# Two token groups take turns with each half of the dense weights, and the third chunk's decays are transferred, in an mLSTM + dense + MoE kernel

## The chip, the cores and the metric

The kernel runs on one core of a Trainium2 chip. The metric is device time in microseconds (us), the median of 3 runs: 747.91 us before the change (747.22 to 748.08). Engines: TensorE (PE) multiplies matrices, VectorE (DVE) and ScalarE (ACT) work elementwise and read PSUM, GpSimd (POOL) works elementwise on SBUF, SyncE (SP) issues most transfers. Each engine runs its own list of instructions in order, and a program of semaphores makes it wait for the others.

## The reference

Three stages follow one another; the output of each is the input of the next.

```python
for t in range(S):                      # 4 batches, 8 heads, 768 steps, head_dim 40
    m_new = max(f[t] + m, i[t]); f_stab = exp(f[t] + m - m_new); i_stab = exp(i[t] - m_new); m = m_new
    C = f_stab * C + i_stab * outer(v[t], k[t])
    n = f_stab * n + i_stab * k[t]
    y[t] = sigmoid(o[t]) * (C @ q[t]) / max(|n . q[t]|, 1)
x = y as 3072 tokens x 320
x = relu(x @ w_in) ** 2 @ w_out         # 320 x 2048, 2048 x 320
e = argmax(x @ w_gate); p = softmax(x @ w_gate)[e]        # 8 experts
out = p * (relu(x @ w1[e]) @ w2[e])     # 320 x 1024, 1024 x 320
```

All data are float32. The dense weights are stored by the host as packed 64-bit words.

## The kernel before

**Attention.** The 3072 tokens are 24 chunks of 128 (4 batches of 6). `order` puts the first chunks of batches 0, 1 and 2 at the head (AT_ONCE = 3), then the rest batch by batch. Within a chunk the recurrence is written as products: scores of keys with queries (`scores`, line 774, into sp), times the decays Ab (`weigh`, 779), times values (`values`, 787, into pv); for chunks with a predecessor also a product of the queries with the carried state C (`inter`, by `triples`, 713). C is renewed by `update` (713), `update_masked` (813) and `carried` (line 820 on), which takes its factor from decT. `divided`, `gated`, `turned` and `out` finish the chunk; the last two transpose it and split it into high and low columns xh and xl (733, 734).

**Decays.** Ab needs the running sum A of the log gates. `gate_stage` computes it in two parts, the first chunk of each batch (early) and the rest (late), from two loads of the gates (463, 483), and writes it to DRAM (A_d, 508). From the third place on the decays come back by a transfer that spreads one row over 128 partitions (`decays`, 648), and `causal` subtracts and masks them on POOL (669, 670); `decay` takes the exponential on ACT. For the first AT_ONCE chunks `decays_early` builds the same in PSUM with PE instead (656, 660, 662). The carried factors decT go through DRAM as well: eAL, L_d (521 to 523), and three transfers on SP in `carry` (529), the word dt.

**Dense layer.** Eight token groups g of three chunks meet 16 weight slices f; a pair (g, f) is a unit. Its first layer is 8 matmuls 128x384 (line 859, into hp), then ACT squares (867, 868) and DVE forms the low part (876, 879); its second layer is 9 matmuls 128x320 (892 to 894) into three accumulators in PSUM. Group 0 goes through all f, then group 1, and so on (`its`). At the last f of a group `fin` copies the accumulators out on ACT (974) and does the routing.

**Weights.** For each f, `decode` has a load (A, line 546), a rescaling (R, ACT), a type conversion (T, 562 on POOL, 564 on ACT), the sign (S, 574), the words (W, 578), the high part (H, 582) and the low part (L, 585, on POOL or DVE).

**Order.** PLAN is a list of words written by hand: g a piece of the gate stage, A R T S W H L a decoding turn, kv qk de ca cb ea eb vw the preparation of a chunk, sc wa wb va vb and so on the steps of `Main`, l and m the first and second layer of a unit, sa, sb and sbP its late steps (P on POOL), f a number of filler matmuls (1403). Each word issues its instructions at once, so the list sets the order on all engines. It covers 18 first layers and 16 second layers. After it a loop goes on by a pace: `attend`, called twice in each unit, adds STEP = 9/16 half steps of attention, and a chunk has PERIOD = 6 half steps. The five PSUM buffers of `psa` are shared by hp, sp, pv, Ap and the transposes; the keys and queries st, and kvo, have two buffers each, Ab four.

**Experts.** From 520 us on the routed experts run (lines 96 to 374), which the change does not touch.

Of the kernel before, what the change touches and what calls it, by code (L numbers as in the profile page):

```python
# [25 lines left out]
L = 128  # L26
# [28 lines left out]
FETCH = 2  # L55
# [322 lines left out]
def kernel(ctx, tc, qk, q3, kvo, gates, w_io, wg, w12, cst, out, dbg=None):  # L378
# [41 lines left out]
    L_d = dram.tile([HR, NCH], F32, name="L_d")  # L420
# [3 lines left out]
    decT = const.tile([120, 12, NCH], F32, name="decT")  # L424
# [6 lines left out]
    xrl = const.tile([128, 3, XR], F32, name="xrl")  # L431

# [25 lines left out]
    def gate_stage():  # L458
# [25 lines left out]
        yield  # L484

        def columns(src, dst, c0, c1):
            pt = psa.tile([128, 512], F32, tag="a", name="pt")
            for ch in range(c0, c1):
                nc.tensor.transpose(out=pt[:, HR * ch:HR * ch + HR], in_=src[:, L * ch:L * ch + L], identity=ident[0:HR, 0:HR])
            nc.scalar.activation(out=dst[:, c0:c1], in_=pt[:, HR * c0:HR * c1].rearrange("p (c h) -> p c h", h=HR), func=ACTF.Copy)  # L490

        for k, (part, c0, c1) in enumerate(((early, 0, 1), (late, 1, NCH))):
# [18 lines left out]
            if k:  # L511
                columns(c, cT, 0, NCH)
# [94 lines left out]
    class Chunk:  # L607
# [958 lines left out]
```

## Time and profile before

| | |
|---|---|
| median of 3 runs | 747.91 us |
| the profiled execution, its time | 745.5 us |
| its span | 743.7 us |
| PE busy | 731.1 us (98%) |
| weight loads of PE busy | 718.0 us (97%) |
| DVE busy | 500.8 us (67%) |
| ACT busy | 418.1 us (56%) |
| POOL busy | 358.2 us (48%) |
| transfers | 108.99 MB, mean 147 GB/s |

The span goes from the first to the last instruction that the hardware profiler records; the time has what lies around it as well. Busy time is the time in which an engine executes, without register, branch, semaphore and transfer-issuing instructions. Matmuls overlap, so that the durations of single records may add up to more than the time they take together; a row of the chain of waits gives the time that a piece of work holds on the path that ended last. An idle time is put down to what ended it. PE's granted clock is given as a share of its full speed.

### The profile page before, as it was taken

Reading aid. Unit: us, or ns where it says so; the run is one execution under the profiler, and the core shown is the slowest. Engines: PE = TensorE matmul, PEld = TensorE weight load, DVE = VectorE, ACT = ScalarE, POOL = GpSimd, SP = SyncE. Lnnn points to the kernel's source line nnn. Section 1 sums busy time; section 2 is a strip of 40 time slices with the busy share of each in tenths; the row PEclk is TensorE's granted clock in tenths of the full one; section 3 lists DMA queues with packets and bytes.
Section 4 is the critical chain, followed back from the end, with each engine's and each line's share of the span. In section 5 each row is a group of like instructions: output and inputs, shape, how many; then the busy total and the mean of one; then the engine's idle time right before and its main releaser. Section 6 shows DMA issues by size and latency. Waiting matters only on the chain.

```text
span 743.7 us, 14447 instructions
## 1 busy us (share of the span) xinstructions
PE 731.1 (98%) x5198; PEld 718.0 (97%) x5198; DVE 500.8 (67%) x1140; ACT 418.1 (56%) x807; POOL 358.2 (48%) x411
## 2 busy tenths in 40 slices
PE   9999999999999999999999999999999999999996
PEld 6899999999999999999999999999899999999996
DVE  9899874875866776575685664455475767877563
ACT  5687865555455456455455434663374566776553
POOL 8568755555455355265355401531346325666431
PEclk9999999999999999999999999999999999999999
DMA  8788864567354364264364000100297556777610
GB/s 253 230 241 270 244 160 106 144 169 239 102 148 119 87 163 121 56 190 115 92 181 100 25 34 1 34 34 34 82 353 234 145 185 201 254 226 243 183 43 24
DMA packets 55043, 108.99 MB, mean 147 GB/s; under 512 B 6896, under 2 KB 34681, under 8 KB 54834
## 3 DMA queue, kind: packets, MB, share of 16 engines
q1 hardware_dynamic: 50370, 95.88, 44.5%
q0 software_dynamic: 4160, 11.77, 5.0%
q8 instruction: 47, 0.77, 0.4%
q10 hardware_dynamic: 432, 0.29, 0.1%
q14 instruction: 34, 0.28, 0.1%
HBM read 98.69 MB, written 10.86 MB: 147 GB/s over the span
## 4 chain that ended last, share of the span: by engine, by line
PE 95%; DVE 3%; issue 1%; ACT 0%; POOL 0%; POOLq 0%; DVEq 0%; SPq 0%
PE hp L859 25%; PE hp L292 13%; PE acc L892 8%; PE acc L894 8%; PE acc L893 8%; PE pv L787 5%; PE op L311 4%; PE op L313 4%; PE op L312 4%; PE sp L774 4%; PE tp L713 3%; PE lp L957 2%; PE xp L278 1%; PE lpt L948 1%; PE xpt L723 1%; PE apart L1403 1%
## 5 line engine op out<-in xcount | busy, mean ns | idle before, releaser
L641 POOL TENSOR_TENSOR kq<-st,kq 120x256 fp32r<-120x256 f32 x136 | 96.6, 742 | 140.6 <-ACT kq L638 140.6
L892 PE MATMUL acc<-w_h,gh 128*128 128x320 f32 x384 | 125.0, 326 | 0.0
L867 ACT ACTIVATE g<-hp 128x384 f32<-128x384 f32 x128 | 62.3, 487 | 102.9 <-PE hp L859 102.3
L894 PE MATMUL acc<-w_h,gl 128*128 128x320 f32 x384 | 118.6, 309 | 0.0
L893 PE MATMUL acc<-w_l,gh 128*128 128x320 f32 x384 | 118.2, 308 | 0.0
L876 DVE SCALAR_TENSOR_TENSOR hp<-hp,g 128x384 f32<-128x384 f32 x126 | 70.6, 560 | 67.3 <-ACT g L867 67.0
L859 PE MATMUL hp<-xh,w_h 128*128 128x384 f32 x384 | 111.9, 345 | 1.6 <-DVE xh L734 1.6
L261 DVE SCALAR_TENSOR_TENSOR gl<-hp,gh 128x384 fp32r<-128x384 f32 x88 | 48.0, 556 | 59.2 <-ACT gh L231 58.6
L859 PE MATMUL hp<-xh,w_l 128*128 128x384 f32 x384 | 87.4, 335 | 0.0
L859 PE MATMUL hp<-xl,w_h 128*128 128x384 f32 x256 | 86.5, 338 | 0.0
L879 DVE TENSOR_TENSOR gl<-hp,gh 128x384 fp32r<-128x384 f32 x126 | 70.3, 558 | 14.3
L893 PEld LDWEIGHTS acc<-w_l,gh 128*128 128x128 f32 x384 | 72.4, 189 | 0.0
L892 PEld LDWEIGHTS acc<-w_h,gh 128*128 128x128 f32 x384 | 72.4, 188 | 0.0
L894 PEld LDWEIGHTS acc<-w_h,gl 128*128 128x128 f32 x384 | 72.0, 188 | 0.0
L868 ACT ACTIVATE gh<-g 128x384 fp32r<-128x384 f32 x128 | 67.3, 525 | 4.4 <-PE acc L893 0.4
L859 PEld LDWEIGHTS hp<-xh,w_l 128*128 128x128 f32 x384 | 68.9, 188 | 0.0
L859 PEld LDWEIGHTS hp<-xh,w_h 128*128 128x128 f32 x384 | 65.5, 189 | 1.8 <-ACT signs L564 1.8
L231 ACT ACTIVATE gh<-hp 128x384 fp32r<-128x384 f32 x88 | 43.2, 491 | 39.7 <-PE hp L292 38.8
L638 ACT ACTIVATE kq<-st,cs 120x1024 fp32r<-120x1024 f32 x34 | 39.0, 1148 | 33.7 <-PE sp L774 33.7
L174 POOL DMA_INDIRECT out_dram<-ot,idx x34 | 41.8, 1231 | 25.7 <-ACT ot L210 18.5
L676 ACT ACTIVATE Ab<-Ab 128x512 f32<-128x512 f32 x42 | 26.2, 628 | 44.4 <-POOL Ab L670 44.4
L787 PEld LDWEIGHTS pv<-kvo,Ab 128*128 128x128 f32 x384 | 48.4, 191 | 0.5
(291 smaller groups left out, 1837.0 us busy)
## 6 DMA issues: line engine op xcount, KB each, us to landing
st<-in_qk_dram SPq DMA_DIRECT2D x34, 480.0 KB
raw<-in_w_dram SPq DMA_DIRECT2D x30, 512.0 KB, 4.6
kvo<-in_kvo_dram SPq DMA_DIRECT2D x24, 529.0 KB
raw<-in_w_io_dram SPq DMA_DIRECT2D x16, 704.0 KB
Ab<-A_d SPq DMA_DIRECT2D x42, 256.0 KB
raw<-in_w_dram SPq DMA_DIRECT2D x20, 427.0 KB, 3.4
raw<-in_w_dram SPq DMA_DIRECT2D x10, 426.0 KB, 4.7
q<-in_q_dram SPq DMA_DIRECT2D x20, 180.0 KB
```

The source lines that it names most:

```text
L261: e.scalar_tensor_tensor(out=gl[:, j], in0=hp[j % 4], scalar=0.0, in1=gh[:, j].bitcast(F32), op0=ALU.max, op1=ALU.subtract).then_inc(sGL, 1)
L292: m = e.matmul(hp[f % 4][:, 0:w], a, c, start=(n == 0), stop=(n == 7))
L641: nc.gpsimd.tensor_tensor(out=o[:, c], in0=self.st[j][:, c], in1=o[:, c].bitcast(F32), op=ALU.subtract)
L787: nc.tensor.matmul(self.pv[:, hd], d.Ab[r][:, i], d.v[:, hd], start=True, stop=True)
L859: nc.tensor.matmul(hp, a, x, start=(n == 0), stop=(n == 7))
L867: nc.scalar.activation(out=r, in_=hp, func=ACTF.Relu)
L868: nc.scalar.activation(out=gh, in_=r, func=ACTF.Square)
L876: e.scalar_tensor_tensor(out=sq, in0=hp, scalar=0.0, in1=r, op0=ALU.max, op1=ALU.mult)
L879: e.tensor_tensor(out=gl, in0=sq, in1=gh.bitcast(F32), op=ALU.subtract)
L892: nc.tensor.matmul(acc[t][:, 0:DM], gh[:, sl], wh, start=(f == 0), stop=False)
L893: nc.tensor.matmul(acc[t][:, 0:DM], gh[:, sl], wl, start=False, stop=False)
L894: nc.tensor.matmul(acc[t][:, 0:DM], gl[:, sl], wh, start=False, stop=end)
```

## The change

1. The units of groups 0 and 1 (SHARED = 2) come in four blocks of PART = 8: (0, f 0 to 7), (1, f 0 to 7), (0, f 8 to 15), (1, f 8 to 15). At f = 7 of both, ACT copies the accumulators to rows of xr2 or xrl, and at f = 15 DVE adds to these rows what the accumulators then hold.
2. `decays_early` is used for ON_PE = 2 chunks where it was for three; the third chunk's decays come through `decays` and `causal`. For that, the first column block of cT is transposed in the early part of the gate stage.
3. decT is made by a product on DVE (own), one matmul on PE and a copy on ACT, from constants that one more small load brings; L_d and `carry` go.
4. PLAN is written anew and covers 26 first layers and 24 second layers; it has 22 filler matmuls where 21 stood. Up to unit 32 the pace is QUICK = 5/4 a call of `attend`.
5. FETCH, the group at whose first unit the first expert's weights are loaded, is 3 where it was 2.

```diff
-FETCH = 2
+FETCH = 3
+ON_PE = 2
+SHARED, PART, QUICK = 2, 8, 5 / 4
 PLAN = """
-    g0 g1 A0 R0 qk0 g2 g3 A1 kv0 TP0 g4 g5 g6 f7 de0 ea0 g7 eb0 g8 R1 g9 TP1 A2 S0 sc0 de1 th0 g10 W0 vw0 qk1 H0 SA1 ea1 R2 up0 A3 eb1 TP2 g11 wb0 wa0 g12
+    g0 A0 g1 g2 R0 kv0 g3 qk0 g4 TQ0 g5 A1 f7 g6 de0 ea0 f3 g7 g8 g9 qk1 S0 W0 sc0 vw0 eb0 g10 A2 H0 g11 R1 wa0 kv1 wb0 de1 T1 S1 th0 ea1 va0 vb0 eb1 R2
...
-    L_d = dram.tile([HR, NCH], F32, name="L_d")
-    decT = const.tile([120, 12, NCH], F32, name="decT")
+    decT = const.tile([120, 3 * B, NCH - 1], F32, name="decT")
+    rows3, rows12 = xrl[0:HR, 1, 0:120], xrl[0:HR, 1, 120:120 + 3 * B]
+    own = xrl[0:HR, 1, 132:132 + 3 * B * (NCH - 1)].rearrange("p (g c) -> p g c", c=NCH - 1)
...
+        nc.scalar.dma_start(out=xrl[0:HR, 1, 0:120 + 3 * B], in_=cst[0:HR, 521 + TT:])
-        def columns(src, dst, c0, c1):
+        def columns(src, dst, c0, c1, more=None):
...
+            if more:
+                more(pt)
...
             if k:
-                columns(c, cT, 0, NCH)
+                columns(c, cT, 1, NCH)
+            else:
+                columns(c, cT, 0, 1)
...
-        columns(eA, eAT, 1, NCH)
-        eAL = const.tile([HR, NCH], F32, name="eAL")
-        nc.vector.memset(eAL[:, 0:1], 0.0)
-        nc.vector.tensor_copy(out=eAL[:, 1:NCH].rearrange("p (c o) -> p c o", o=1), in_=chunked(eA)[:, :, L - 1:L])
-        nc.gpsimd.dma_start(out=L_d, in_=eAL)
+        nc.vector.tensor_tensor(out=own, in0=rows12.rearrange("p (g o) -> p g o", o=1).to_broadcast([HR, 3 * B, NCH - 1]),
+                                in1=chunked(eA)[:, :, L - 1:L].rearrange("p c o -> p o c").to_broadcast([HR, 3 * B, NCH - 1]), op=ALU.mult)
+        pt = columns(eA, eAT, 1, NCH, lambda pt: nc.tensor.matmul(pt[0:120, 256:256 + 3 * B * (NCH - 1)], rows3, own.rearrange("p g c -> p (g c)"), start=True, stop=True))
+        nc.scalar.activation(out=decT.rearrange("p g c -> p (g c)"), in_=pt[0:120, 256:256 + 3 * B * (NCH - 1)], func=ACTF.Copy)
...
         def causal(self, j):
-            if self.n < AT_ONCE:
+            if self.n < ON_PE:
                 return
...
-            wh, wl, end = w_h[:, f, 384:IO], low_of(f)[:, 384:IO], f == NF - 1
+            wh, wl, begin, end = w_h[:, f, 384:IO], low_of(f)[:, 384:IO], f % PART == 0 and (f == 0 or g < SHARED), f == NF - 1 or (g < SHARED and f == PART - 1)
...
         def rows(t):
-            nc.scalar.activation(out=xr[:, t, 64:384], in_=acc[t][:, 0:DM], func=ACTF.Copy)
+            if g < SHARED:
+                nc.vector.tensor_tensor(out=xr[:, t, 64:384], in0=acc[t][:, 0:DM], in1=xr[:, t, 64:384], op=ALU.add)
+            else:
+                nc.scalar.activation(out=xr[:, t, 64:384], in_=acc[t][:, 0:DM], func=ACTF.Copy)
...
-        its = [(g, f) for g in range(NG) for f in range(NF)] + [(NG, f) for f in range(NF0)]
+        its = [(g, f) for p in (0, PART) for g in range(SHARED) for f in range(p, p + PART)] + [(g, f) for g in range(SHARED, NG) for f in range(NF)] + [(NG, f) for f in range(NF0)]
...
-            pace[0] += STEP
+            pace[0] += STEP if nl[0] > SHARED * NF else QUICK
...
-            if f == 0:
+            if f == 0 or (g < SHARED and f == PART):
                 accs[g] = accumulators()
...
+            if g < SHARED and f == PART - 1:
+                for t, acc in enumerate(accs.pop(g)):
+                    nc.scalar.activation(out=(xrl if g % 2 else xr2)[:, t, 64:384], in_=acc[:, 0:DM], func=ACTF.Copy)
```

The changed kernel's line numbers are 4 to 10 higher at the places shown. Three places show how it moves instructions. The first is PE between the scores of the second chunk and those of the third: sp are scores, xpt transposes of a finished chunk, Ap the decays built on PE (Ap<-scr and the two products of line 660 and 662 for each half), apart fillers, tp a product of `triples`. The kernel before:

```order
L774 MATMUL sp<-kqs 128x128 x8
L721 MATMUL xpt<-cs,kvo 64x128
L723 MATMUL xpt<-cs,kvo 128x128 x2
L656 LDWEIGHTS scr
L656 MATMUL Ap<-scr 128x512
L656 LDWEIGHTS scr
L656 MATMUL Ap<-scr 128x512
L660 MATMUL Ap<-flat,cs 128x128 x4
L662 MATMUL Ap<-cs,flat 128x512
L660 MATMUL Ap<-flat,cs 128x128 x4
L662 MATMUL Ap<-cs,flat 128x512
L774 MATMUL sp<-st 128x128 x8
```

The changed kernel, from the row behind the second chunk's scores to the third's:

```order
L494 MATMUL pt<-cs,flat 128x36 x5
L725 MATMUL xpt<-cs,kvo 64x128
L727 MATMUL xpt<-cs,kvo 128x128 x2
L717 MATMUL tp<-vw,kvo 120x126 x3
L1413 LDWEIGHTS ones
L1413 MATMUL apart<-ones 128x512
L1413 LDWEIGHTS ones
L1413 MATMUL apart<-ones 128x512
L1413 LDWEIGHTS ones
L1413 MATMUL apart<-ones 128x512
L791 MATMUL pv<-kvo,Ab 128x42 x8
L778 MATMUL sp<-st 128x128 x8
```

The third chunk's block is gone there, and transposes of the gate stage (pt), an update, fillers and values (pv) stand in its place.

The second place is POOL before the first dense matmul, from the type conversions (line 562) on; L669 and L670 (673 and 674 after) are `causal`. The kernel before:

```order
L562 TENSOR_SCALAR raw<-raw 128x704
L499 TENSOR_TENSOR flat<-scr,flat 36x640
L562 TENSOR_SCALAR raw<-raw 128x704
L682 TENSOR_TENSOR vw<-kvo,wT 128x378
L562 TENSOR_SCALAR raw<-raw 128x704
L585 TENSOR_TENSOR w_l<-raw,w_h 128x704 x3
L682 TENSOR_TENSOR vw<-kvo,wT 128x378
L585 TENSOR_TENSOR w_l<-raw,w_h 128x704
L682 TENSOR_TENSOR vw<-kvo,wT 128x378
L523 DMA L_d<-eAL 36x6
L585 TENSOR_TENSOR w_l<-raw,w_h 128x704
L669 TENSOR_TENSOR Ab<-Ab,cT 128x512
```

The changed kernel:

```order
L507 TENSOR_TENSOR flat<-scr,flat 36x640
L686 TENSOR_TENSOR vw<-kvo,wT 128x378 x2
L673 TENSOR_TENSOR Ab<-Ab,cT 128x512
L674 AFFINE_SELECT Ab<-Ab 128x512
L673 TENSOR_TENSOR Ab<-Ab,cT 128x512
L674 AFFINE_SELECT Ab<-Ab 128x512
L589 TENSOR_TENSOR w_l<-raw,w_h 128x704
L686 TENSOR_TENSOR vw<-kvo,wT 128x378
L673 TENSOR_TENSOR Ab<-Ab,cT 128x512
L674 AFFINE_SELECT Ab<-Ab 128x512
L673 TENSOR_TENSOR Ab<-Ab,cT 128x512
L674 AFFINE_SELECT Ab<-Ab 128x512
```

The `causal` operations of the third and of the fourth chunk stand here now, and most conversions and low parts have left this stretch.

The third place is the head of SP's queue. Line 463 and 483 load the two parts of the gates, 546 weights, 628 keys and queries, 617 kvo, 508 writes A. The kernel before, from its first transfer on:

```order
L463 DMA scr<-in_gates_dram 36x256
L483 DMA scr<-in_gates_dram 36x1280
L926 DMA x_d<-xrl 1x392
L546 DMA raw<-in_w_io_dram 128x1408
L628 DMA st<-in_qk_dram 40x1024 x2
L546 DMA raw<-in_w_io_dram 128x1408
L617 DMA kvo<-in_kvo_dram 128x1058
L508 DMA A_d<-flat 36x128
L546 DMA raw<-in_w_io_dram 128x1408
L628 DMA kqs<-in_qk_dram 40x1024 x2
L546 DMA raw<-in_w_io_dram 128x1408
L508 DMA A_d<-flat 36x640
```

The changed kernel, from its second transfer on (the first is again the first part of the gates):

```order
L550 DMA raw<-in_w_io_dram 128x1408
L930 DMA x_d<-xrl 1x392
L487 DMA scr<-in_gates_dram 36x1280
L621 DMA kvo<-in_kvo_dram 128x1058
L632 DMA st<-in_qk_dram 40x1024 x2
L516 DMA A_d<-flat 36x128
L550 DMA raw<-in_w_io_dram 128x1408
L632 DMA kqs<-in_qk_dram 40x1024 x2
L550 DMA raw<-in_w_io_dram 128x1408
L516 DMA A_d<-flat 36x640
L621 DMA kvo<-in_kvo_dram 128x1058
L652 DMA Ab<-A_d 128x4x128 x2
```

The second part of the gates is now behind a load of weights, three loads of weights stand where four stood, and the two transfers of the third chunk's decays (652) follow the second kvo.

## Rows read from the trace of the kernel before

**Rows 1.** Stretches: us, then busy us (count) by engine, clock, DMA share, GB/s.

```profile
0.00:40.00 40.00, 37.31 (x295) 29.50 (x296) 35.87 (x61) 23.29 (x40) 27.92 (x33) 1.00 0.80 245
40.00:520.00 480.00, 479.69 (x3403) 476.92 (x3401) 320.47 (x839) 265.54 (x538) 225.89 (x298) 1.00 0.44 122
105.40:164.60 59.20, 58.93 (x418) 58.47 (x418) 38.49 (x109) 30.16 (x60) 29.83 (x43) 1.00 0.53 140
```

**Rows 2.** Waits of PE, 0 to 330: us in total, times, longest.

```profile
PE hp L859 <- DVE xh L734: 1.6, 1, 1.6
PE pr L1024 <- DVE oh L1018: 0.3, 1, 0.3
```

**Rows 3.** The chain that ended last, in order of time: start us, us.

```profile
23.28 0.43 PE Ap L656 x2
23.71 0.89 PE Ap L660 x8
24.60 0.86 PE Ap L662 x2
...
27.21 1.79 PE sp L774 x16
...
31.07 0.65 PE apart L1403 x3
...
38.35 7.20 PE hp L859 x40
...
51.95 0.67 PE tp L713 x6
...
105.68 1.41 PE hp L859 x8
```

**Rows 4.** Timelines of DVE, ACT, POOL: start us, us, [idle before <-releaser].

```profile
5.83 1.54 DVE L496 TENSOR_TENSOR_SCAN flat<-scr,flat 36x640 f32<-36x640 f32 x1
...
7.33 0.86 ACT L551 ACTIVATE raw<-raw 128x704 f32<-128x704 f32 x1 [4.38 <-DMA raw<-in_w_io_dram]
...
22.08 1.69 POOL L585 TENSOR_TENSOR w_l<-raw,w_h 128x704 fp32r<-128x704 f32 x1 [3.16 <-ACT w_h L581]
...
22.34 2.17 DVE L578 SCALAR_TENSOR_TENSOR raw<-raw 128x704 int32<-128x704 int32 x1
...
27.17 0.89 DVE L578 SCALAR_TENSOR_TENSOR raw<-raw,signs 128x704 int32<-128x704 int32 x1
...
34.48 0.17 DVE L826 TENSOR_SCALAR den<-pv 128x8 f32<-128x8 f32 x1 [1.56 <-PE pv L787]
...
36.29 0.55 DVE L813 TENSOR_TENSOR U<-tp,cs 120x378 f32<-120x378 f32 x1
...
37.92 0.28 DVE L734 TENSOR_TENSOR xh<-xpt,xh 64x128 fp32r<-64x128 f32 x1
```

**Rows 5.** Groups of POOL by line, 100 to 420: busy us, mean ns, idle before.

```profile
L669 POOL TENSOR_TENSOR Ab<-Ab,cT 128x512 f32<-128x512 f32 x32 | 33.6, 1049 | 0.0
L670 POOL TENSOR_SCALAR_AFFINE_SELECT Ab<-Ab 128x512 f32<-128x512 f32 x32 | 20.4, 636 | 2.4
```

**Rows 6.** Timeline of PE at the end of group 0: start us, us.

```profile
104.20 0.31 PE L892 MATMUL acc<-w_h,gh 128*128 128x320 f32 x1
...
105.52 0.51 PE L859 MATMUL hp<-xh,w_h 128*128 128x384 f32 x2
```

**Rows 7.** Line 974: ns min/median/max, first and last start us.

```profile
L974 ACT ACTIVATE xr<-acc x12: 421/430/440, 105.4 to 456.8; 128x320 f32<-128x320 f32 x12
L974 ACT ACTIVATE xrl<-acc x12: 410/431/441, 164.6 to 506.0; 128x320 f32<-128x320 f32 x12
```

**Rows 8.** Waits of SP's queue, 100 to 330: us in total, times, longest.

```profile
SPq L628 <- POOL kq L641: 65.3, 21, 4.1
```

**Rows 9.** The page: a group of part 5, a transfer of part 6.

```profile
L638 ACT ACTIVATE kq<-st,cs 120x1024 fp32r<-120x1024 f32 x34 | 39.0, 1148 | 33.7 <-PE sp L774 33.7
...
raw<-in_w_dram SPq DMA_DIRECT2D x30, 512.0 KB, 4.6
```

More of the change, by code (lines that the diff above doesn't have):

```diff
@@ L76 @@
+    ou6 kv7 sa24 l25 sb24 sa25 sb25
 """.split()
@@ L672, in decay @@
         def decay(self, j):
-            if self.n < AT_ONCE:
+            if self.n < ON_PE:
                 self.Ab[j] = at4.tile([128, 4, L], F32, tag="Ab", name="Ab")
             Ab = self.Ab[j]
-            nc.scalar.activation(out=Ab, in_=Ab if self.n >= AT_ONCE else self.Ap[j], func=ACTF.Exp)
+            nc.scalar.activation(out=Ab, in_=Ab if self.n >= ON_PE else self.Ap[j], func=ACTF.Exp)
         def weighted(self):
@@ L706, in ahead @@
             over.add((m, name, *a))
-            assert name != "decay" or m < AT_ONCE or (m, "causal", *a) in over
-            getattr(chunks[m], "decays_early" if name == "decays" and m < AT_ONCE else name)(*a)
+            assert name != "decay" or m < ON_PE or (m, "causal", *a) in over
+            getattr(chunks[m], "decays_early" if name == "decays" and m < ON_PE else name)(*a)
     def triples(np_, lhs, rhs):
@@ L819, in carried @@
                 for g in range(3):
-                    nc.vector.scalar_tensor_tensor(out=C[:, g], in0=C[:, g], scalar=decT[:, 3 * self.b + g, self.c:self.c + 1], in1=self.U[:, g], op0=ALU.mult, op1=ALU.add)
+                    nc.vector.scalar_tensor_tensor(out=C[:, g], in0=C[:, g], scalar=decT[:, 3 * self.b + g, self.c - 1:self.c], in1=self.U[:, g], op0=ALU.mult, op1=ALU.add)
         def divided(self):
@@ L885, in l2 @@
             assert decoded(f)
-            wh, wl, end = w_h[:, f, 384:IO], low_of(f)[:, 384:IO], f == NF - 1
+            wh, wl, begin, end = w_h[:, f, 384:IO], low_of(f)[:, 384:IO], f % PART == 0 and (f == 0 or g < SHARED), f == NF - 1 or (g < SHARED and f == PART - 1)
         else:
             wh, wl = w0[0][:, W1 + DM * f:W1 + DM * f + DM], w0[2][:, DM * f:DM * f + DM]
-            end = f == NF0 - 1
+            begin, end = f == 0, f == NF0 - 1
         for t in ts:
             sl = slice(L * t, L * t + L)
-            nc.tensor.matmul(acc[t][:, 0:DM], gh[:, sl], wh, start=(f == 0), stop=False)
+            nc.tensor.matmul(acc[t][:, 0:DM], gh[:, sl], wh, start=begin, stop=False)
             nc.tensor.matmul(acc[t][:, 0:DM], gh[:, sl], wl, start=False, stop=False)
@@ L1418, in token @@
             else:
[L1419 removed]
+                {"z": constants}[name]()
         for _ in range(APART):
@@ L1542, in _pack @@
     cst[:,393:521]=(p[:,None]<p[None,:])
-    cst[:,521:]=[C*b+c for b in range(AT_ONCE) for c in (0,)]+[C*b+c for b in range(B) for c in range(C) if c or b>=AT_ONCE]
+    r=_np.arange(3*B*3)
+    for j in range(3): cst[r[r%3==j],521+TT+40*j:561+TT+40*j]=1.0
+    cst[r,641+TT+r//3]=1.0
+    cst[:,521:521+TT]=[C*b+c for b in range(AT_ONCE) for c in (0,)]+[C*b+c for b in range(B) for c in range(C) if c or b>=AT_ONCE]
     return dict(qk=qk,q3=q3,kvo=kvo,gates=gates,w_io=w_io,wg=wg,w12=w12,cst=cst)
```

25 lines of the change are left out of this document (11 added, 14 removed).

## The prediction

> **What bounds the kernel now.** I read the busy times over stretches first [rows 1]. From 40 to 520 us, which is all of the dense layer and most of the attention, TensorE (PE) is busy 479.69 of 480.00 us, VectorE (DVE) 320.47, ScalarE (ACT) 265.54, GpSimd (POOL) 225.89. The reader is to see that nothing can be gained there on another engine: the time is the sum of PE's instructions. The list of PE's waits says the same from the other side [rows 2]: up to 330 us, once it has begun, it stood idle twice, 1.6 us before a matmul of line 859, and 0.3 us. The first 40 us are different: PE is busy 37.31 us, but DVE 35.87, so two engines run almost level [rows 1]. The 1.6 us is the wait before the very first dense matmul, which the chain of waits puts at 38.35 us [rows 3]; the last operation it needs, a column split on DVE, ends at 37.92 + 0.28 = 38.20 us [rows 4]. So an edit after 38 us is worth its PE time, and one before it only as much as the later of PE and DVE gives up.
>
> **The change, part by part**, against the profiled execution of 745.5 us, whose span is 743.7.
>
> *Third chunk's decays by transfer.* PE loses one decays_early: in the chain two first products of 0.43 us, two groups of 0.89 and two of 0.86 [rows 3], together 0.43 + 1.78 + 1.72 = 3.93 us. The work comes back as two 256 KB loads on SP's queue, and on POOL two adds and two selects of 1.049 and 0.636 us, 3.37 us [rows 5]; ACT's two exponentials stay, with a buffer in SBUF as source. On SP's queue the loads wait until PE has read the first chunk's Ab buffers, and behind them stand the third chunk's keys and queries, the fourth weight load and the third kvo; the kernel before had five weight loads issued by then, but units that share weights need them half as fast. Term: **-3.93**.
>
> *One filler more.* PLAN has 22 filler matmuls where 21 stood; three take 0.65 us [rows 3], one 0.22. Term: **+0.22**.
>
> *The carried decays by a matmul.* Three small transfers on SP and one on POOL's queue leave, and on PE one matmul of 60 columns comes in. The trace has none. The nearest row is the product with C, three matmuls of 126 columns in 0.67 us [rows 3], 0.22 each; the new one lies between 0 and that, half as wide, and since a narrow one need not cost half I take 0.15. DVE gets a product of 36 x 60 for two small copies, ACT one copy of 60 columns and the issue of one small load. The transposes of cT are split, not added to. Term: **+0.15**.
>
> *The wait at the first dense matmul.* In the new order the fourth chunk's scores and its product with C stand ahead of that matmul; they are moved, not added: 1.79 + 0.67 = 2.46 us [rows 3]. PE alone would arrive there at 38.35 - 1.6 - 3.93 + 0.22 + 0.15 + 2.46 = 35.65 us. For DVE I counted what stands ahead of the same point in the two orders: operations on 128x704 words of line 574 are 2 instead of 4, those of line 578 3 instead of 5; one low part of the same shape comes in, and one masked update. With the 0.89 of an undisturbed word operation for each of the first three and 0.55 for the update [rows 4] that is -1.78 - 1.78 + 0.89 + 0.55 = -2.1. DVE also stood 1.56 us waiting for PE at 34.48 [rows 4], behind products that PE now reaches earlier. So it could end at 38.20 - 1.56 - 2.1 = 34.5. Against that, the second load of the gates now stands behind the first weights on SP's queue; before, the scan of these gates began at 5.83 us, while ACT began on the first weights, on landing, at 7.33 [rows 4]. That is a delay of 0 to 1.5 us, so DVE ends between 34.5 and 36.0. Since the two engines must also alternate, I put the first dense matmul at 36.3: 0.7 of the 1.6 us of wait are left. Term: **-0.9**; bounds -1.6 and, by the first rival, +2.4.
>
> *Sharing the weights.* The order of units becomes eight weights for group 0, the same eight for group 1, then the other eight twice. Number and shape of the matmuls stay. Weights need decoding half as often, but PE did not wait for weights in this stretch [rows 2], so that by itself buys nothing. What it adds is two boundaries at which the three accumulators are emptied: six ACT copies, 0.43 us each [rows 7], and DVE adds in place of six others. At a boundary of before, three such copies begin at 105.4 [rows 7], and PE goes on at 105.52 with a layer-one block [rows 6] and does not wait [rows 2]. Of the new boundaries one has two layer-one blocks and a product as cover, the tight one a single block, 1.41 us [rows 3], against 3 x 0.43 = 1.29; but the second and third bank are needed later than the first. I take nothing, at most 0.5 for both.
>
> *Steps written out, and the quick pace.* After PLAN, up to layer-one unit 32, the planner does 2.5 half steps of attention per unit, where it did 1.125. Nothing is added, but two chunks go through more quickly, and POOL comes close to PE (second rival). For waits there and at the boundaries I take **+0.4**, with bounds 0 and 2.5. FETCH only moves the load of the first expert's weights to a later unit; PE's work from 520 us on is untouched.
>
> Sum: -3.93 + 0.22 + 0.15 - 0.9 + 0.4 = **-4.1 us**, so 741.4 for the profiled execution, which lies 2.4 under the median of the runs, 747.91. The median becomes **743.9**.
>
> **A rule that speaks against it.** While POOL ran line 585 from 22.08 to 23.77 us, an operation of line 578 on DVE, begun at 22.34, took 2.17 us; the same operation takes 0.89 at 27.17 [rows 4]. The rest of POOL's time, 23.77 - 22.34 = 1.43, and 0.89 would be 2.3. So a DVE operation beside one of POOL can lose nearly as much as POOL has left. The Trainium skill, page "SBUF — State Buffer", section "SBUF: two separate sides", has it that a DVE operation with two inputs in SBUF and a GpSimd operation that reads SBUF take a port pair they share as an exclusive lock, the loser standing still for all of the other. This trace agrees (2.17 against 0.89). By that rule the moved decays could hold DVE for all of their time.
>
> **The rivals.**
>
> *DVE is held up and keeps the first 38 us (no change).* Four POOL operations for the third chunk, and likewise four for the fourth, now stand before the first dense matmul. If the third chunk's four hold up DVE for their whole length, DVE ends 3.37 us later, the first dense matmul comes at 36.3 + 3.37 = 39.7, and of the sum -0.7 is left: **747.2**. A load that lands too late, with PE idle where the block stood, would give the same. For it: the 2.17 us above. Against it: much of DVE's work there reads PSUM, and POOL loses three conversions and, at 1.69 us each [rows 4], low parts from the same stretch. 0.12.
>
> *The quick stage starves PE (slower).* A group of three chunks takes 59.2 us, from the first evacuation at 105.4 to that at 164.6 [rows 7], and in it POOL works 29.83 [rows 1], 9.9 a chunk. PE has 16 units in it; a layer-one block is 1.41 us [rows 3], and the nine matmuls of a second-layer step go from 104.20 to 105.52, 1.32 [rows 6], so a unit is 2.73 and 16 are 43.7, which leaves (59.2 - 43.7) / 3 = 5.2 us of attention a chunk. At 2.5 half steps a unit and six to a chunk, a chunk is 2.4 units: 2.4 x 2.73 + 5.2 = 11.7 us of PE against 9.9 of POOL. But SP loads the next keys and queries only when POOL has done with the buffer; it waited 65.3 us in 21 waits for that [rows 8]. A 512 KB load took 4.6 us to land and ACT's scaling takes 1.15 [rows 9]. If both stood in line with POOL's work, a chunk would take 9.9 + 5.75 = 15.7 us, 4.0 over PE, and two chunks 8: -4.1 + 7.9 = +3.8, **751.7**. It decides from about 14.5 us a chunk, where two chunks cost the 5.6 us that turn -4.1 into +1.5. Against it: there are two buffers, and between two uses of one POOL has the other half's work to do. 0.07.
>
> *More than forecast.* The waits of 1.6 and 0.3 us vanish and none comes in: -3.56 - 1.6 - 0.3 = -5.5, **742.4**. 0.16.
>
> **How the numbers follow.** The forecast, -4.1, has 0.62, and by its bounds runs from -5.5 to about -1.5. With "more" at 0.16, no change at 0.12, slower at 0.07 and 0.03 for what isn't listed (part of it on each side), faster by over 0.2% (1.5 us, about what a measurement of this kernel can tell from no change) gets 0.62 + 0.16 + 0.02 = 0.80, within it 0.12, slower 0.08. The range for 8 in 10 takes in "more" with 0.4 to spare and the forecast's bounds up to the mild end of the lock, and leaves out the starved stage: 742.0 to 747.0.
>
> **What would show each step.** In the trace of the changed kernel: the products of lines 660 and 662 for two chunks instead of three; the first dense matmul between 35.6 and 37 us with less than 1 us of wait before it; PE without gaps over the evacuations at about 75, 98 and 118 us; POOL nearly full in the 30 us after PLAN while PE stays at 20.0 of 20 us; the dense layer's end, and with it all that follows, about 4 us earlier. The prediction is wrong if PE waits more than 2 us between 20 and 40 us, for DVE or a load, or as much after 120 us for POOL; or if the span shrinks while the dense stretch does not move.

## The result and the profile after

The changed kernel takes **755.83 us** (754.62 to 758.62), the kernel before 748.0 beside it: a ratio of **1.0111**, 95% interval 1.0082 to 1.014. It is slower by 1.1%; 743.9 was forecast, and 747.0 was the upper end.

The profiled execution took 755.73 us, its span is 753.9. That of before had been 2.4 us under its median, this one lies on it, so the two spans differ by 10.2 us where the medians differ by 7.8. Up to the first matmul of the experts (line 292 before, 295 after; 533.9 and 541.4 us) the changed kernel loses 7.5 us. The expert part behind it takes 209.8 before and 212.5 after, but 210.1 in on_pe3 below, which has the same code there. I therefore look for the loss in the first 541 us.

Busy time over stretches, of the changed kernel (columns as in [rows 1]):

```profile
0.00:40.00 40.00, 37.94 (x308) 30.78 (x309) 32.20 (x60) 22.66 (x42) 21.54 (x32) 1.00 0.82 242
40.00:120.00 80.00, 80.00 (x554) 79.81 (x553) 67.47 (x120) 61.95 (x106) 54.52 (x59) 1.00 0.63 190
120.00:200.00 80.00, 72.84 (x507) 71.19 (x507) 50.72 (x152) 35.94 (x70) 40.19 (x60) 0.96 0.51 137
200.00:520.00 320.00, 320.00 (x2251) 318.17 (x2251) 191.72 (x539) 166.38 (x358) 137.03 (x189) 1.00 0.36 102
```

The reader is to see one bad stretch. In the first 40 us DVE has 32.20 busy us for 35.87 of before [rows 1], PE 37.94. From 40 to 120 and from 200 on PE is full. From 120 to 200 it stands still for 7.2 of 80 us, and its granted clock, 1.00 everywhere else, is 0.96 there. The kernel before has 79.73 busy us in that stretch at a clock of 1.00:

```profile
120.00:200.00 80.00, 79.73 (x571) 79.05 (x571) 54.30 (x161) 39.40 (x77) 37.97 (x56) 1.00 0.52 152
```

PE's waits up to 520 us in the changed kernel (for [rows 2]):

```profile
PE sp L778 <- ACT scr L956: 3.9, 1, 3.9
PE pr L1031 <- DVE gl L883: 1.6, 1, 1.6
PE apart L1432 <- POOL ones L909: 1.0, 1, 1.0
PE lpt L952 <- DVE so L1041: 0.7, 1, 0.7
PE xpt L725 <- DVE gl L883: 0.7, 1, 0.7
PE sp L778 <- DMA st<-in_qk_dram: 0.5, 2, 0.4
PE pt L531 <- DVE xrl L529: 0.5, 1, 0.5
```

The wait for xh before the first dense matmul is gone. New are 3.9 us before scores, two of 1.6 and 0.7 before the routing's matmuls, 0.65 before a transpose at 155.95 us, and at the head about a microsecond in three small ones. The same PE, over the stretches around the two large ones:

```profile
134.00:139.00 5.00, 1.06 (x8) 0.90 (x8) 1.17 (x3) 2.28 (x5) 3.36 (x5) 0.96 0.60 146
139.00:142.00 3.00, 3.00 (x14) 3.00 (x15) 2.85 (x6) 1.02 (x3) 0.00 (x0) 0.50 0.68 162
...
170.00:173.00 3.00, 0.67 (x10) 0.54 (x9) 2.73 (x11) 0.20 (x1) 0.58 (x1) 0.96 0.68 159
173.00:176.00 3.00, 3.00 (x13) 3.00 (x12) 2.90 (x13) 0.49 (x1) 0.00 (x0) 0.50 0.00 0
```

Behind each of them PE works for a little over 3 us at a granted clock of 0.50, the lower level of 1.2 GHz. Second-layer matmuls start 0.27 us apart there and 0.15 us apart elsewhere, so about 1.5 us are lost each time (an estimate from these spacings).

**The first wait, followed back.** The timelines of POOL, ACT and PE (start, duration, work, and in brackets the idle time before it and who ended it):

```profile
127.64 2.82 POOL L645 TENSOR_TENSOR kq<-st,kq 120x256 fp32r<-120x256 f32 x4 [6.54 <-ACT kq L642]
130.40 1.06 POOL L673 TENSOR_TENSOR Ab<-Ab,cT 128x512 f32<-128x512 f32 x1
131.54 0.63 POOL L674 TENSOR_SCALAR_AFFINE_SELECT Ab<-Ab 128x512 f32<-128x512 f32 x1
132.14 2.80 POOL L645 TENSOR_TENSOR kq<-st,kq 120x256 fp32r<-120x256 f32 x4
134.90 1.04 POOL L673 TENSOR_TENSOR Ab<-Ab,cT 128x512 f32<-128x512 f32 x1
136.02 0.63 POOL L674 TENSOR_SCALAR_AFFINE_SELECT Ab<-Ab 128x512 f32<-128x512 f32 x1
...
136.68 0.63 ACT L680 ACTIVATE Ab<-Ab 128x512 f32<-128x512 f32 x1 [3.84 <-POOL Ab L674]
137.22 0.47 ACT L871 ACTIVATE g<-hp 128x384 f32<-128x384 f32 x1
137.72 0.52 ACT L872 ACTIVATE gh<-g 128x384 fp32r<-128x384 f32 x1
138.15 0.47 ACT L956 ACTIVATE scr<-lpt 128x384 f32<-128x384 f32 x1
...
134.00 0.83 PE L717 MATMUL tp<-C,q 120*128 120x126 f32 x6
138.77 1.08 PE L778 MATMUL sp<-kq 120*128 120x128 f32 x4 [3.94 <-ACT scr L956]
```

Read it from the end. PE is done at 134.83 and wants a PSUM buffer for scores. That buffer holds transposes of the routing, which ACT copies out at 138.15 (line 956). The copy stands in ACT's queue behind the second exponential of the next chunk's decays (680), and that waits 3.84 us for a mask on POOL which ends at 136.65. The split keys and queries themselves (645) were ready at 134.94, 0.1 us after PE. So POOL, busy for two splits and two masks in a row, is late by 1.8 us, and ACT's queue passes this on to work that has nothing to do with it. The row begins at 127.64 because POOL had nothing for 6.54 us: ACT scaled the keys of chunk 8 only behind the scores of chunk 7, since kq has one buffer. (How much of the 6.54 us that buffer makes, kq_apart8 below shows: 2.1.)

**The second.** DVE works on a part of group 0's routing, the three adds of group 1, and the attention's and the dense layer's steps in one row; PE's transposes and prefix sums wait for it:

```profile
168.21 1.28 DVE L979 TENSOR_TENSOR xrl<-acc,xrl 128x320 f32<-128x320 f32 x3
...
171.12 0.56 DVE L883 TENSOR_TENSOR gl<-hp,gh 128x384 fp32r<-128x384 f32 x1
...
172.52 0.15 DVE L1041 TENSOR_TENSOR so<-cum,oh 128x8 bf16<-128x8 bf16 x1
...
171.73 0.17 PE L1031 MATMUL pr<-oh,tri 128*128 128x24 bf16 x1 [1.60 <-DVE gl L883]
172.75 0.87 PE L952 MATMUL lpt<-cs,xrl 128*128 128x128 f32 x3 [0.73 <-DVE so L1041]
```

**The head** went nearly as forecast. The timeline's first dense matmul, the product ahead of it, and the new matmul of the carried decays:

```profile
33.01 0.41 PE L531 MATMUL pt<-xrl 36*120 36x60 f32 x2 [0.46 <-DVE xrl L529]
...
36.08 0.83 PE L717 MATMUL tp<-C,q 120*128 120x126 f32 x6
36.73 0.59 PE L863 MATMUL hp<-xh,w_h 128*128 128x384 f32 x2
```

36.73 us for 38.35 [rows 3], with 2.46 us of moved work ahead of it: 4.1 us gained. These are single executions: in the kernels below that have the same head it lies between 36.2 and 37.75 us, but for kq_apart_fin. The decays' products on PE are for two chunks now, 32 and 8 records for 48 and 12.

So the account is: -4.1 at the head, 6.9 us of waits (3.94 + 0.65 + 1.60 + 0.73) and 3.0 of half clock behind it make 5.8; where the last 1.7 of the 7.5 come from isn't shown.

### The profile page after: what moved, and what is told of

Same layout as the page of the kernel before. It is cut to its first block, busy times and chain, and to the rows that moved or that the text cites. A ratio compares the mean times of both kernels' runs of the same rounds, so it can differ in the third digit from the quotient of the medians.

```text
span 753.9 us, 14422 instructions
## 1 busy us (share of the span) xinstructions
PE 731.4 (97%) x5178; PEld 717.9 (95%) x5179; DVE 493.0 (65%) x1140; ACT 418.7 (56%) x809; POOL 357.1 (47%) x419
## 4 chain that ended last, share of the span: by engine, by line
PE 88%; DVE 4%; issue 3%; POOL 2%; DMA 2%; ACT 1%; SPq 0%; POOLq 0%; DVEq 0%
PE hp L863 23%; PE hp L295 13%; PE acc L896 8%; PE acc L898 8%; PE acc L897 7%; PE pv L791 5%; PE op L314 4%; PE op L316 4%; PE op L315 4%; PE sp L778 3%; PE tp L717 3%; PE lp L961 2%; PE xp L281 1%; PE lpt L952 1%; POOL kq L645 1%
## 5 line engine op out<-in xcount | busy, mean ns | idle before, releaser
L880 DVE SCALAR_TENSOR_TENSOR hp<-hp,g 128x384 f32<-128x384 f32 x121 | 67.8, 560 | 74.4 <-ACT g L871 74.3
L883 DVE TENSOR_TENSOR gl<-hp,gh 128x384 fp32r<-128x384 f32 x121 | 67.5, 558 | 14.3 <-ACT gh L872 0.7
```

The source lines that it names most:

```text
L880: e.scalar_tensor_tensor(out=sq, in0=hp, scalar=0.0, in1=r, op0=ALU.max, op1=ALU.mult)
L883: e.tensor_tensor(out=gl, in0=sq, in1=gh.bitcast(F32), op=ALU.subtract)
```

## The experiments

Times are medians of the run; ratios are to the kernel before on the same chip, with 95% intervals. Chips differ, so kernels of different runs are compared by ratio. "First expert matmul" is the time at which the part that the change concerns ends, in the profile: 533.9 before, 541.4 changed. Each profile is one execution on its run's chip.

**Where the head's gain comes from.** on_pe3 undoes one part in the changed kernel:

```diff
-ON_PE = 2
+ON_PE = 3
```

> The changed kernel, but the third chunk's decays are built on PE again (ON_PE 3). Theory: the head of the changed kernel gains what was forecast and the loss lies behind it, so undoing this part costs its PE time, 3.9 us: about 759.7. Rival, that the transferred decays are what holds DVE or PE at the head: undoing costs nothing or gains, 754 to 756.

758.32 us, 1.0142 (1.0125 to 1.0159), 0.3% above the changed kernel; first dense matmul at 40.8 us for 36.7, first expert matmul at 546.6. The 4.1 us at the head are there in full, and 5.2 at the end of the dense part; the median shows 2.5 of them, since the expert part is 2.4 us shorter in this kernel's profile. The 5.2 hold more half clock too: PE works at it for over 5 us behind the wait at the scores. That wait is 4.2 us here, so the loss behind doesn't depend on this part.

b_on_pe2 does the same part alone in the kernel before (line 648's transfer for the third chunk, its masks ca2 and cb2 written before ea2):

```diff
+ON_PE = 2
-            if self.n < AT_ONCE:
+            if self.n < ON_PE:
...
-    va2 eb2 th2
+    ca2 cb2 ea2 W4 wa2 f3 va2 eb2 th2
```

> The kernel before with one part of the change alone: the third chunk's decays by transfer and POOL (ON_PE 2), everything else in the old order. Theory: before the first dense matmul DVE leads, so the 3.9 us that PE loses turn into a longer wait there (1.6 becomes 4 to 5 us) and only what DVE itself waited for PE, up to 1.6 us, can come back: 746.3 to 748. Rival, that PE leads and the removal is worth itself: 744.

750.28 us, 1.004 (1.0021 to 1.0059): no gain, even a small loss. In the profile, which is of its fastest execution (747.5), the first dense matmul comes at 38.8 us, 0.4 later than before. PE's waits there:

```profile
PE hp L860 <- DVE xh L735: 1.5, 1, 1.5
PE sp L775 <- DMA st<-in_qk_dram: 1.4, 1, 1.4
PE pv L788 <- DMA kvo<-in_kvo_dram: 0.9, 1, 0.9
PE xpt L722 <- DVE kvo L834: 0.6, 1, 0.6
```

The removed 3.9 us became waits for DVE, and, which I hadn't expected, for keys, queries and kvo. Removing PE work at the head is worth something only together with the new order of loads and of DVE's work.

**What starves PE behind PLAN.** b_quick puts the quick pace alone into the kernel before, without shared weights:

```diff
-            pace[0] += STEP
+            pace[0] += STEP if nl[0] > 32 else 5 / 4
```

> The kernel before with the quick pace alone: 2.5 half steps of attention per unit up to unit 32 instead of 1.125, no shared weights. Theory: the pace by itself puts the splits of keys and queries, the masks and the exponentials in a row that PE has to wait for, several us in one or two places between 100 and 160 us: 750 to 754. Rival, that the waits need the shared order with its two routings close together: 748 within 1.

762.75 us, 1.0197 (1.0168 to 1.0226). Its waits:

```profile
PE sp L774 <- ACT scr L952: 3.9, 1, 3.9
PE sp L774 <- DVE gl L879: 3.4, 1, 3.4
```

and, over a stretch:

```profile
110.00:130.00 20.00, 16.07 (x100) 15.82 (x100) 7.32 (x16) 9.67 (x19) 10.33 (x14) 0.83 0.62 163
```

The same wait of 3.9 us for the same copy, with the same exponential ahead of it in ACT's queue (3.86 us for POOL's mask, ending at 120.4). So the pace makes it, without the sharing. The cost is above what I had put down, up to 754: the pace also brings a second large wait and more half clock.

quick1 slows the pace in the changed kernel (QUICK 1 for 5/4).

> The changed kernel with a quick pace of 2 half steps of attention per unit instead of 2.5 (QUICK 1); what is then missing of chunks 7 and 8 is issued in one piece before unit 32, which needs their tokens. Theory: the shared order needs two chunks in six units whatever the pace, so the waits only move towards unit 32: 755 to 758. Rival, that the number of half steps per unit makes the wait: 751 to 753.

765.11 us, 1.0149 (1.0124 to 1.0175) beside a slower chip's 752.96. Neither expectation holds. The 3.9 us become 1.8, but now group after group waits for its tokens:

```profile
PE hp L863 <- DVE xh L738: 9.4, 7, 2.1
PE hp L863 <- ACT scr L956: 1.8, 1, 1.8
```

Seven waits of 0.8 to 2.1 us up to 464 us: attention that falls behind in the quick stage stays behind for the rest of the layer. The shared order has two groups' units done by unit 32, as before, but needs group 1's tokens at unit 8 for 16; whether another PLAN could serve it without a quick stage, no run tests.

decay_late moves the exponential that blocks ACT:

```diff
+        if n + 1 < 3 * (SHARED + 1):
+            todo[5].append(todo[4].pop())
```

> The changed kernel, but up to chunk 8 the planner issues the second exponential of the next chunk's decays one half step later. Theory: in the quick stage ACT stands at that exponential until POOL's mask of 136.65 us is done, and behind it in ACT's queue stand two squares and the copy of line 956 that gives PE its PSUM buffer; then the PE wait of 3.9 us falls under 1.5 and the time to about 752 (-2.5 and -1.3 of clock). Rival, that POOL itself is too late whatever stands in ACT's queue: the wait only moves, 755.8 within 0.8.

750.23 us, 1.0034 (1.0015 to 1.0053); first expert matmul at 535.3, 6.1 us earlier. The wait of 3.9 is one of 1.0, and the clock is 1.00 from 120 to 200 us although the 1.6 and 0.7 at 166 us are still there. A better result than expected, since the half clock behind the second place went too.

kq_apart8 takes the first link away: chunk 8's split keys and queries get the slots of the unsplit ones, and those go to raw, which the weights no longer need.

```diff
-                self.kq = at1.tile([120, 2, H * L], F32R, tag="kq", name="kq")
+                if self.n in (8,):
+                    self.kq = [at2.tile([120, H * L], F32R, tag="st", name="kq") for _ in range(2)]
...
+            if self.n in (8, 9):
+                x = raw[0:120, WN - 2 * H * L * (2 - self.n % 2):][:, 0:2 * H * L]
```

> As kq_apart, but only chunk 8 has the buffer of its own and chunk 10's load is where it was, so that the 4.2 us that kq_apart brought in at 174 us, for a load of keys and queries, can't come from this edit. Theory, as the wait in kq_apart already fell from 3.9 to 1.9 us without half clock: 2 + 1.7 us less than the changed kernel's 755.8, about 752. Rival, that the split only comes earlier and ACT stands longer at the next exponential: 755 or more.

754.1 us beside 752.96, 1.0025 (1.0004 to 1.0045). POOL begins the row 2.1 us earlier (timeline), with 4.51 us of its 6.54 idle us left, and those are not the buffer's: ACT begins that scaling at 124.28, right behind squares of the dense layer. The wait is 2.0 us shorter (list of waits), and the clock behind it stays at 1.00:

```profile
125.50 2.84 POOL L652 TENSOR_TENSOR kq<-raw,kq 120x256 fp32r<-120x256 f32 x4 [4.51 <-ACT kq L649]
```

```profile
PE sp L785 <- ACT scr L963: 2.0, 1, 2.0
```

An earlier form, kq_apart, gave chunk 10 such a buffer as well.

> The changed kernel (755.8), but the split keys and queries of chunks 8 and 10 have a buffer of their own (the slots of the unsplit ones, which go to the idle weight buffer), so that their split needn't wait until PE has done the scores of the chunk before. Theory: POOL's idle stretch of 6.5 us before 127.6 us, in which ACT waits for those scores, is the start of the wait at 134.8; without it the 3.9 us of PE and the 1.7 us of half clock go: about 750. Rival, that the order in ACT's queue alone makes the wait (the exponential ahead of the copy, as decay_late showed): it stays over 2.5 us, 754 or more.

756.83 beside 752.69, 1.0059 (1.0034 to 1.0083): the wait fell to 1.9 us, but chunk 11's load then had to wait for chunk 10's scores, and PE stood 4.2 us at 174.

k8_decay has both edits, kq_apart8's and decay_late's.

> kq_apart8 and the second exponential one half step later (decay_late, 750.2). Theory: both edits act on the same wait at 134.8, by its start and by its last link, so together they gain little over the better one: 749.5 to 750.5. Rival, that they act on different waits and add up: 747 or less.

751.08 beside 752.96, **0.9984** (0.9969 to 1.0); first expert matmul at 533.6. Neither wait is left at 134 to 139 us, PE has 39.82 of 40 us from 120 to 160. In ratios decay_late took 0.8% off, kq_apart8 0.9%, both together 1.3%: they are links of one chain, as the wait shows, but one removes 3 of its 3.9 us and the other 2, so that together they do gain over either. "Little over the better one" was wrong.

whole9 takes the splits away altogether for chunks 7 and 8 (WHOLE 9 for 7).

> The changed kernel (755.8 us), but chunks 7 and 8 use their keys and queries unrounded, as the first seven do (WHOLE 9 for 7), so that POOL has no splits of 0.74 us for them, 16 in all, and PE does their scores in the slower form. Theory: the 3.9 us that PE stands at 134.8 to 138.8 us and the half clock behind it come from POOL being late in the quick stage; then that wait is gone (-3.9, -1.3 of clock), PE pays about 2 x 0.9 us more for scores: about 752.5. Rival, that the wait comes from ACT or DVE work of the two routings and POOL is only beside it: the wait stays, and with the slower scores the time is about 757.6.

751.4 us, 1.0044 (1.003 to 1.0057): the wait is gone, two of 0.4 for POOL are left, the 1.6 and 0.7 stay, and the slower scores cost what was expected.

pool_first does both splits before both masks, with both exponentials later, and group 0's routing twice as fast:

```diff
+        if n + 1 < 11:
+            todo[2], todo[3], todo[4], todo[5] = [], todo[2], todo[4][:1] + todo[3], [todo[4][1]] + todo[5]
```

> The changed kernel with group 0's routing two steps per unit, and up to chunk 10 another order in the quick stage: POOL does both splits of a chunk's keys and queries before the two masks, and both exponentials come one half step later. Theory: PE's scores wait for the splits and ACT's queue for the masks, so the rest of the waits at 138 and 151 us (1.0 and 0.4 in decay_late) goes too: 746.5 to 747.5. Rival, that the later masks hold DVE's products with the decays and so PE's values: 749 or more.

753.58 us, 1.0077 (1.0058 to 1.0097). The scores no longer wait, but the first exponential now waits 4.63 us for its mask, and the copy of line 958 behind it makes PE wait 2.1: the same chain by its other exponential. It is slower than 749, as the rival had it, but not by the rival's way.

**The routing's waits.** fin_later delays group 1's routing by six units:

```diff
+                if g == 1:
+                    q = delayed(q)
```

> The changed kernel, but the routing of group 1 after its evacuation starts six units later than it did, so that it no longer follows directly on that of group 0. Theory: the waits of 1.6 and 0.7 us of PE at 170 to 173 us, with the half clock behind them (1.3), come from DVE, which has the rest of group 0's routing, three adds of group 1 and the dense and attention work in one row: they go, about 752.3. Rival, that the adds alone hold DVE: the waits stay within 0.5 us, 755.5.

754.67 us, 1.0087 (1.007 to 1.0104). The 0.7 went and the clock behind it stayed at 1.00; the 1.6 stayed as it was. So the 1.6 us don't come from group 1's routing following on group 0's, as the theory had it.

decay_fin has decay_late's edit and issues group 0's routing two steps a unit.

```diff
+            for _ in q:
+                next(q, None)
+                yield
```

> The changed kernel with the second exponential one half step later (up to chunk 8, as in decay_late, 750.2) and the routing of group 0 issued two steps per unit, so that it is over before group 1 is evacuated. Theory: the waits of 1.6 and 0.7 us at about 166 us come from group 0's routing, the adds of group 1 and the dense and attention work standing in one row on DVE; they go, about 748. Rival, that DVE has too little time there in whatever order: they move to another matmul, 750.

749.55 us, 1.0017 (1.0004 to 1.0031); first expert matmul at 535.3, as in decay_late. The rival: the 1.6 us came back at 150 us before a dense matmul, for the routing on DVE.

k8_decay_fin puts the same edit on k8_decay.

> k8_decay, and the routing of group 0 two steps per unit as in decay_fin. Theory: the 1.6 and 0.7 us go, but a part comes back at about 150 us, as the 1.6 us for DVE in decay_fin: 0.996 to 0.999 of before. Rival, that nothing comes back now that the splits are earlier: 0.994.

748.03 beside 748.77, 0.9992 (0.9979 to 1.0006); first expert matmul at 533.3 for 533.6. Of the 2.3 us at 165 us 0.8 are left, and 0.5, 0.4 and 0.6 us are new at 140 to 153. The ratio lies just above the theory's range.

k8_decay_rows takes the adds off DVE instead:

```diff
-                nc.vector.tensor_tensor(out=xr[:, t, 64:384], in0=acc[t][:, 0:DM], in1=xr[:, t, 64:384], op=ALU.add)
+                nc.scalar.activation(out=half2, in_=acc[t][:, 0:DM], func=ACTF.Copy)
+                nc.gpsimd.tensor_tensor(out=xr[:, t, 64:384], in0=half2, in1=xr[:, t, 64:384], op=ALU.add)
```

> k8_decay (0.998 of the kernel before), and the accumulators of groups 0 and 1 leave at the end by an ACT copy into a free buffer and an add on POOL instead of an add on DVE. Theory: the waits of 1.6 and 0.7 us that are left at 164 to 166 us come from DVE's row of routing, adds and dense work; without the 1.3 us of adds the 1.6 falls under 0.7 and PE's time by 1 to 2.3 us: 0.995 to 0.997 of before. Rival, that the routing alone fills DVE there, or the sum now comes too late for group 1's transposes: 0.998 or more.

746.46 us beside 748.77, **0.9979** (0.9958 to 0.9999): faster than both kernels, if barely clear of the one before. Its ratio lies between the theory's 0.997 and the rival's 0.998, and the intervals don't tell it from k8_decay's 0.9984. First expert matmul at 531.6, 2.3 us before that of the kernel before. The 1.6 us are gone: they need the adds. They need group 0's routing too, for decay_fin and k8_decay_fin lost them at this place by a quicker routing. With one wait of 0.7 us left, 2.3 us are still less than the 4.1 of the head; what holds the rest isn't shown either. Stretches, and the one wait left over 0.2 us from 100 to 200:

```profile
120.00:160.00 40.00, 39.86 (x291) 39.17 (x291) 26.02 (x70) 22.52 (x44) 30.40 (x44) 1.00 0.57 143
160.00:200.00 40.00, 39.25 (x287) 38.87 (x286) 31.01 (x101) 20.63 (x42) 22.54 (x34) 1.00 0.53 143
```

```profile
PE lpt L961 <- DVE kvo L846: 0.7, 1, 0.7
```

Two runs had trouble of their own. kq_apart_fin (kq_apart and the quicker routing) and whole9_fin (whole9, decay_late's edit and the quicker routing):

> As kq_apart, and the routing of group 0 two steps per unit (the edit of decay_fin). Theory: the two edits act in different places, so the 1.6 and 0.7 us at 170 us and the half clock behind them go as well: 746.5 to 748, level with the kernel before or just under it. Rival, that the quicker routing brings waits of its own, as the 1.6 us for DVE at 150 us in decay_fin: 749 to 750.

> As whole9 (751.4: the scores of chunks 7 and 8 from unsplit keys and queries), with the second exponential later and the routing of group 0 two steps per unit. Theory: of the waits only 0.7 us are left and the 2.8 us of half clock behind 170 us go: 747 to 748, with 1.8 us more of scores on PE. Rival: the waits of the routing move, as in decay_fin, 749 to 750.

764.02 beside 752.69, 1.0145 (1.0119 to 1.0171), and 758.73, 1.0071 (1.0046 to 1.0097). The first has the 4 us of kq_apart, and in its profile half clock from about 26.5 to 43.5 us, behind a wait of 0.9 us for keys and queries that ends at 25.9; its first dense matmul is at 44.4. That profile is of its slowest execution, 773.44 us. The second ends the dense part at 537.9, 1.7 us earlier than whole9, but its expert part took 221.3 us in the profile, where the others have 210 to 217. No edit touches that part; why it is longer there stays open, and these two decide nothing.

## Why the prediction was wrong

- **Third chunk's decays, -3.93: right.** 4.1 us at the first dense matmul, and 4.1 when it is undone. But alone it gives nothing (b_on_pe2): the reading that PE and DVE run level at the head was right, though loads took their share of the new waits, and the term holds only with the rest of the new order.
- **One filler, +0.22: right in kind, with no row that prices it alone. The matmul of the carried decays, +0.15: a little small.** The timeline's 0.41 us can't be compared with the term, which came from the chain of waits. Where it lies on that chain, in whole9_fin, it holds 0.23 us, just over the upper bound of 0.22: half as many columns were not cheaper. What the term left out is the wait of 0.46 us for DVE's product ahead of it.

```profile
32.61 0.23 PE pt L531 x2
```

- **The wait at the first dense matmul, -0.9: right in kind.** The first dense matmul stood at 36.7, forecast 36.3, with no wait directly ahead of it; 0.8 us of waits lie a little earlier, at 25 and 33 us. The rival with DVE held up for 3.37 us didn't happen: DVE's busy time in the first 40 us fell by 3.7 us. In small it did, as the last point shows.
- **Sharing the weights, 0 to 0.5: wrong step.** The accumulators were emptied without a wait, as said. What I costed at nothing were the adds on DVE, for which the prediction has only the words "DVE adds in place of six others". I asked only whether PE's next layer-two unit waits for the banks. The adds' 1.3 us stand in DVE's queue ahead of dense and attention steps that hold PSUM buffers, beside group 0's routing, which now falls eight units before group 1's end: 2.3 us of waits and 1.5 of half clock. k8_decay_rows shows that the 1.6 of them go with the adds.
- **The quick pace, +0.4 with bounds 0 to 2.5: the step that failed.** It cost 4.6 us of waits (3.94, and the 0.65 at 155.95, which is gone in kq_apart8) and 1.5 of half clock. It is the second rival's place, and near its size: the rival gave 751.7 and a chance of 0.07, and with the 3.8 us of the routing on top one is near 755.8. The nearness is in part luck, as the rival put a load and ACT's scaling in line with POOL's work for 7.9 us, and nothing of half clock or of ACT's queue behind an exponential. I priced it so low for two reasons that the runs disprove. I compared POOL's 9.9 us with PE's 11.7 as if only throughput counted; but POOL, forecast nearly full behind PLAN, was busy 21.52 of the 40 us from 120 to 160 and PE waited all the same. The chain goes from scores to scaling to split, mask, split, mask, exponential, and on to whatever stands behind the exponential in ACT's queue, and it is passed once a chunk. And I held against it that "there are two buffers": that is so for the unsplit keys and queries, while the split ones have one, and 2.1 of POOL's 6.5 us without work come from that (2 us of the wait in kq_apart8). ACT as a link, the larger one (3 us in decay_late), was nowhere in my working: it was busy 265 of 480 us, and I took that as room.
- **Half clock: missing.** No row of before shows PE's clock falling in this stretch, since PE hardly waited there, and I priced a wait at its own length only. Here the waits, 6.9 us in all, cost 3.0 more.
- **The rule on the shared ports: at work, but small.** DVE had less to do at the head, not more. But its new product of the carried decays ran beside a mask of the fourth chunk, one of those that now stand at the head, took 0.95 us, and ended 0.11 us after it; PE's wait of 0.46 us at 33.01 is for this product. In k8_decay_fin it began 0.02 us ahead of the mask, and took 0.26. So DVE lost 0.7 us beside that mask, where the rival had 3.37 in all. The two lines of the changed kernel, and the one of k8_decay_fin:

```profile
31.80 1.04 POOL L673 TENSOR_TENSOR Ab<-Ab,cT 128x512 f32<-128x512 f32 x1
32.00 0.95 DVE L529 TENSOR_TENSOR xrl<-xrl,flat 36x60 f32<-36x60 f32 x1 [0.32 <-DMA q<-in_q_dram]
...
32.49 0.26 DVE L529 TENSOR_TENSOR xrl<-xrl,flat 36x60 f32<-36x60 f32 x1 [0.32 <-DMA q<-in_q_dram]
```

Nothing in the sum was of the wrong sign, but the +0.4 for the pace and the nothing for sharing were far too small. It lacked the terms for what a faster supply of attention work does to the queues that make it.

## What to carry to other kernels

Before a change asks one stage to run at twice its rate, follow one unit of that stage through every engine's queue, with each buffer it holds, and add the latencies; busy shares say only that the throughput would do. Where an in-order queue has an operation that waits for a slower engine, ask what unrelated work stands behind it: moving that one operation half a step later was worth 0.8%. And where an engine is full, an edit that moves work off it at one place has to be checked for the place at which the moved order must be caught up.

## What the runs showed of the hardware

PE's granted clock falls to half behind some waits and not behind others of the same length, and how long it stays there differs as well. Behind 3.94 us it was half for a little over 3 us in the changed kernel, behind a like wait of 3.95 in fin_later for over 6, behind 3.92 in b_quick for over 5; behind 1.98 (kq_apart8) it stayed full. The pair of 1.60 and 0.73 us was followed by a little over 3 us of half clock in the changed kernel, by nearly 6 in whole9, and by none in decay_late. In kq_apart_fin's execution PE worked without a gap at half clock for 16 us and more, behind a wait of 0.88. And in whole9_fin no wait in this stretch is longer than 0.4 us, yet PE falls to half clock for over 5 us after it has been busy 1.7 of 3 us. The rows are of fin_later, kq_apart_fin and, from 150 us, whole9_fin:

```profile
140.00:145.00 5.00, 5.00 (x23) 4.91 (x23) 2.69 (x6) 0.76 (x2) 0.00 (x0) 0.50 0.30 82
...
27.00:43.00 16.00, 16.00 (x72) 13.40 (x71) 6.87 (x17) 4.99 (x14) 5.64 (x7) 0.50 0.58 166
...
150.00:151.00 1.00, 0.72 (x6) 0.45 (x4) 0.93 (x3) 0.58 (x2) 1.00 (x2) 1.00 0.08 8
151.00:152.00 1.00, 0.39 (x2) 0.19 (x1) 1.00 (x5) 0.00 (x0) 1.00 (x3) 1.00 0.70 205
152.00:153.00 1.00, 0.55 (x3) 0.41 (x4) 1.00 (x5) 0.00 (x0) 1.00 (x3) 1.00 0.97 250
...
156.00:158.00 2.00, 2.00 (x9) 2.00 (x10) 0.95 (x2) 0.81 (x1) 0.00 (x0) 0.50 0.78 192
```

What decides, these runs don't tell. For a full PE a wait of 2 to 4 us should be priced at its length and up to 3 us more (an estimate: 6 us of half clock, at the spacings above); the 16 us of kq_apart_fin, which put its first dense matmul at 44.4 us for 36.7, show that it can be worse.
